# Dense router scores among the opening products, and balancing sums in the other bank

## The chip, the cores and the metric

The kernel runs on one core of one Trainium2 chip. The metric is the device time of one execution in microseconds, here the median of several runs. PE is TensorE's matmul side, PEld its weight loads, DVE is VectorE, ACT is ScalarE, POOL is GpSimd, SP is the engine that issues the weight DMAs.

## What is computed

Three stages follow one another: linear attention with a decaying state, a first mixture of experts in which each token takes one expert, and a second, dense mixture (`moe2`) in which every token takes all eight experts, weighted by a matrix P that is balanced over rows and columns eight times:

```python
def _moe2_ref(x, w_gate, w1, w2) -> np.ndarray:
    N, D = x.shape
    E = w_gate.shape[1]
    logits = x @ w_gate
    logits = logits - logits.max()
    P = np.exp(logits)
    for _ in range(8):
        P /= P.sum(1, keepdims=True) + 1e-09
        P /= P.sum(0, keepdims=True) + 1e-09
        P *= N / E
    out = np.zeros((N, D), dtype=np.float32)
    for e in range(E):
        h = np.maximum(x @ w1[e], 0.0)
        ye = h @ w2[e]
        out += P[:, e:e + 1] * ye
    return out.astype(np.float32)
```

Here N is 1536, D 512, E 8 and F (the inner size) 1024. `logits` are the dense router's scores; the change concerns how they, and then P, are made.

## The kernel before

The order of work is written by hand: each engine runs its instructions in the order in which the code issues them, and a wait is put where one engine needs another's result. Attention and the first mixture end with the slots of the first mixture (`rest_slot`). The transposed result x stands in two tiles, `x2T[0]` (high parts) and `x2T[1]` (low parts), so that each product of float32 quality is three matmuls: high by high, high by low, low by high (`product`, four blocks of 128 rows of D, so twelve matmuls of 384 columns, lines 780 to 782).

The dense mixture works in groups: half of the tokens, one expert, a quarter of F. Group 0 is `opening`: four products (z = 0 to 3) into banks 6 and 7 of PSUM in turn (`pa`, `pc`), each followed by a `relu` (ACT at line 785, then DVE at line 786) that writes the inner activations `hb`. `opening` stands in both branches of a conditional on the number of slots; the short branch is the one that ran here, and every engine then jumps over the other branch. Groups 1 to 3 are run by `eight`: four steps z, each one product, its `relu`, and then three "triples" of the group before (nine matmuls of 512 columns, lines 969 to 971, which multiply `hb` by the second weights and add up in banks 0 to 5). From group 4 on `seven` does the same with fewer products.

After `opening` the code issues the last weight conversions of expert 0: `conv1(7)` (ACT, then DVE, then a DMA on SP that fetches the second weights into the same staging tile `stg[7]`), then `conv2(4)` to `conv2(7)`, each an ACT copy (line 297) and a DVE difference (line 298). `conv2(7)` needs that DMA. Then come the loads of later weights (line 910) and the dense router:

- `gate_scores(c)`, c = 0 to 2: eight matmuls of 512 columns (line 817) into bank c, and an ACT copy (line 818) of 16 rows into `lgT`, which lies on the tile `snap`.
- `gate_exp`, behind step z = 0 of group 1: twelve "folds" (line 823), matmuls with 16 rows of weights and 8 columns that add high and low scores and turn them into token rows in bank 5. Each is float32 and runs as two passes, so 24 weight loads and 24 matmuls. Then DVE copies them to `Pm` (line 824) and takes the maximum of each row (line 825).
- `gate_peak` (line 829), behind step z = 1: a matmul that turns the maxima into a row, and a DVE maximum.
- `gate_shift` (line 834), behind step z = 2: spreads the maximum; DVE subtracts, ACT takes the exponential, and `balance_rows` (four DVE operations, lines 840 to 843) normalizes rows.
- `balance` (line 849), once behind each step of groups 2 and 3, eight times: a matmul of `ones` by `Pm` (two passes of 96 columns) that writes the column sums into columns 0 to 95 of the bank whose product the step has just made, four DVE operations (lines 850 to 853), and `balance_rows` but for the last.

POOL's first work after the slots is `xwhole` (line 866), sums of x blocks into `snap`. `points` is the table that says what runs behind which step of which group.

Of the kernel before, what the change touches and what calls it, by code (L numbers as in the profile page):

```python
# [15 lines left out]
AF = mybir.ActivationFunctionType  # L16
# [5 lines left out]
C = 128  # L22
NCH = S // C
M = B * NCH
# [92 lines left out]
def build(tc, i, out):  # L117
# [3 lines left out]
    with ctx:  # L121
# [523 lines left out]
        with ExitStack() as st2:  # L645
# [132 lines left out]
            def product(b, w, x, start, stop, kks=2):  # L778
                for kk in range(kks):
                    T.matmul(out=b, lhsT=w(0, kk), rhs=x(0, kk), start=start and kk == 0, stop=False, skip_group_check=True)  # L780
                    T.matmul(out=b, lhsT=w(0, kk), rhs=x(1, kk), start=False, stop=False, skip_group_check=True)  # L781
                    T.matmul(out=b, lhsT=w(1, kk), rhs=x(0, kk), start=False, stop=stop and kk == kks - 1, skip_group_check=True)  # L782

# [5 lines left out]

            def opening():  # L790
                for z in range(4):
                    fi, th = z % 2, z // 2
                    b = (pa, pc)[z % 2][:, 0:HT]
                    product(b, lambda t, kk: w1b[fi][:, t, kk], lambda t, kk: x2T[t][:, kk, th * HT:(th + 1) * HT], True, True, 4)
                    relu(hs[0][fi][th], b)
# [14 lines left out]
            lgT = snap.rearrange("p u t -> p (u t)")[0:2 * NE]  # L810
            rs, cs, gm = tab[:, 430:430 + M], tab[:, 446:446 + NE], tab[:, 458:460]
            ones12 = [128, M, NE]
            def gate_scores(c):
                b = bank[c]
                for t in range(2):
                    for kk in range(4):
                        T.matmul(out=b, lhsT=wg2s[:, kk], rhs=x2T[t][:, kk, c * 512:(c + 1) * 512], start=t == 0 and kk == 0, stop=t == 1 and kk == 3)
                A.activation(out=lgT[:, c * 512:(c + 1) * 512], in_=b[0:2 * NE], func=AF.Copy)

            def gate_exp():  # L820
                b = bank[5]
                for m in range(M):
                    T.matmul(out=b[:, m * NE:(m + 1) * NE], lhsT=lgT[:, m * C:(m + 1) * C], rhs=k("fold")[0:2 * NE], start=True, stop=True)
                V.tensor_copy(out=Pm, in_=b[:, 0:M * NE].rearrange("p (m e) -> p m e", e=NE))
                V.tensor_reduce(out=gm[:, 0:1], in_=Pm, axis=AX.XY, op=ALU.max)
# [21 lines left out]
            def balance(at):  # L847
                b = at[:, 0:M * NE]
                T.matmul(out=b, lhsT=ones, rhs=Pm.rearrange("p m e -> p (m e)"), start=True, stop=True)
                V.tensor_reduce(out=cs, in_=b.rearrange("p (m e) -> p e m", e=NE), axis=AX.X, op=ALU.add)  # L850
                V.tensor_scalar(out=cs, in0=cs, scalar1=1e-9, scalar2=None, op0=ALU.add)
                V.reciprocal(out=cs, in_=cs)
                V.scalar_tensor_tensor(out=Pm, in0=Pm, scalar=float(N) / NE, in1=bc(cs, 1, ones12), op0=ALU.mult, op1=ALU.mult)
                left[0] -= 1
                if left[0]:
                    balance_rows()
# [122 lines left out]
            def eight(n, points):  # L979
# [9 lines left out]
                for z, (fi, th) in enumerate(((0, 0), (1, 0), (0, 1), (1, 1))):  # L989
# [4 lines left out]
                    for _ in range(3):  # L994
                        for fn in (next(todo, None),):
                            if fn:
                                fn()
                    if old and z in (1, 3):
# [13 lines left out]
            def seven(n):  # L1012
# [52 lines left out]
                1: {0: [gate_exp], 1: [gate_peak], 2: [gate_shift]},  # L1065
            }
            for n in range(2, 4):
                points[n] = {z: [lambda z=z: left[0] and balance((pa, pc)[z % 2])] for z in range(4)}
# [11 lines left out]
            for c in range(3):  # L1080
                gate_scores(c)
# [27 lines left out]
```

## Time and profile before

| what | value |
|---|---|
| runs before, us | 1259.06, 1260.19, 1259.06 (median 1259.06) |
| profiled execution, us | 1260.48 |
| its span, us | 1258.7 |
| mean granted TensorE clock | 0.998 of full speed |
| PE busy | 1246.2 us, 99% |
| DVE, ACT, POOL busy | 678.4, 490.9, 423.3 us |
| chain that ended last | PE 96%, DVE 1%, DMA 1%, POOL 1%, issue 1% |

The span is what the trace of the one profiled execution covers; that execution's own time is 1.8 us longer, since some time lies around it. A busy PE is not PE at its peak: matmuls overlap, so the start of one to the start of the next is the measure of what it costs. The stretch of this change lies between 226 and 305 us.

### The profile page before, as it was taken

To read this page: it belongs to the slowest core of one execution; us is meant where nothing else is said; L and a number is where in the kernel's file an instruction comes from. 1 tells how busy PE (TensorE), PEld (TensorE's weight loads), DVE (VectorE), ACT (ScalarE), POOL (GpSimd) and SP (SyncE) were. 2 spreads that over 40 slices of the span, in tenths; PEclk is the share of its full clock that TensorE was granted. 3 is DMA by queue.
4 is the path that set the end of the run, shared out by engine and by line. 5 is a ranking of instruction groups with operands and counts; after the bars stand their busy time and mean duration, and the time that the engine had idled before them with its cause. 6 is when DMAs were issued, how large, how long until landed. Compare 5 with 4: busy or idle time off the path is not lost.

```text
span 1258.7 us, 19258 instructions
## 1 busy us (share of the span) xinstructions
PE 1246.2 (99%) x7284; PEld 1133.8 (90%) x7284; DVE 678.4 (54%) x1319; ACT 490.9 (39%) x981; POOL 423.3 (34%) x411
## 2 busy tenths in 40 slices
PE   8999999999999999999999999999999999999998
PEld 7899999889999999999999999999999999999996
DVE  7787777346545454545454546354545454545453
ACT  2344555313333333444444433343333333333331
POOL 5401010153333333333333347133333333333332
PEclk9999999999999999999999999999999999999999
DMA  8933655301222222222222232122222222222201
GB/s 311 303 115 121 209 183 160 112 1 42 68 67 68 67 68 67 67 67 67 68 68 67 67 101 85 58 68 71 68 70 68 67 65 71 67 67 68 67 26 51
DMA packets 56841, 112.47 MB, mean 89 GB/s; under 512 B 7088, under 2 KB 7344, under 8 KB 56736
## 3 DMA queue, kind: packets, MB, share of 16 engines
q1 hardware_dynamic: 52272, 100.89, 26.1%
q0 software_dynamic: 2304, 7.05, 1.7%
q10 hardware_dynamic: 2160, 3.18, 0.7%
q8 instruction: 60, 0.98, 0.3%
q14 instruction: 45, 0.37, 0.1%
HBM read 104.80 MB, written 6.29 MB: 88 GB/s over the span
## 4 chain that ended last, share of the span: by engine, by line
PE 96%; DVE 1%; DMA 1%; POOL 1%; issue 1%; ACT 0%; POOLq 0%; SPq 0%; DVEq 0%; ACTq 0%
PE banks L971 14%; PE banks L970 14%; PE banks L969 14%; PE banks L781 13%; PE banks L780 13%; PE banks L782 13%; PE banks L327 2%; PE banks L329 2%; PE banks L328 2%; PE banks L657 2%; PE banks L656 2%; PE banks L658 2%; PE banks L524 1%; PE banks L398 1%; PE banks L473 1%; PE banks L503 1%
## 5 line engine op out<-in xcount | busy, mean ns | idle before, releaser
L933 POOL TENSOR_TENSOR w1r<-sraw,w1r 128x1024 fp32r<-128x1024 f32 x56 | 134.5, 2401 | 573.8 <-ACT w1r L932 573.8
L971 PE MATMUL banks<-w2r,hb 128*128 128x512 f32 x750 | 294.8, 393 | 0.0
L970 PE MATMUL banks<-w2r,hb 128*128 128x512 f32 x750 | 294.1, 392 | 0.0
L969 PE MATMUL banks<-w2r,hb 128*128 128x512 f32 x750 | 291.6, 389 | 0.0
L971 PEld LDWEIGHTS banks<-w2r,hb 128*128 128x128 f32 x750 | 140.7, 188 | 29.6
L785 ACT ACTIVATE hb<-snap 128x384 fp32r<-128x384 f32 x168 | 87.8, 523 | 201.8 <-DVE snap L1055 120.1
L780 PE MATMUL banks<-x2T,w1r 128*128 128x384 f32 x464 | 158.1, 341 | 0.0
L970 PEld LDWEIGHTS banks<-w2r,hb 128*128 128x128 f32 x750 | 140.6, 188 | 19.3
L781 PE MATMUL banks<-x2T,w1r 128*128 128x384 f32 x464 | 157.9, 340 | 0.0
L969 PEld LDWEIGHTS banks<-w2r,hb 128*128 128x128 f32 x750 | 140.8, 188 | 19.0
L782 PE MATMUL banks<-x2T,w1r 128*128 128x384 f32 x464 | 156.6, 337 | 0.0
L782 PE MATMUL banks<-xt,w1r 128*128 128x384 f32 x448 | 151.1, 337 | 0.0
L780 PE MATMUL banks<-xt,w1r 128*128 128x384 f32 x448 | 150.8, 337 | 0.0
L781 PE MATMUL banks<-xt,w1r 128*128 128x384 f32 x448 | 150.8, 337 | 0.0
L786 DVE SCALAR_TENSOR_TENSOR hb<-snap,hb 128x384 fp32r<-128x384 f32 x168 | 102.7, 611 | 66.4 <-ACT hb L785 66.4
L786 DVE SCALAR_TENSOR_TENSOR hb<-banks,hb 128x384 fp32r<-128x384 f32 x88 | 49.0, 556 | 158.7 <-ACT hb L785 158.7
L785 ACT ACTIVATE hb<-banks 128x384 fp32r<-128x384 f32 x88 | 43.3, 492 | 211.4 <-PE banks L782 209.6
L298 DVE TENSOR_TENSOR w2r<-stg,w2r 128x512 fp32r<-128x512 f32 x150 | 103.4, 691 | 4.8 <-ACT w2r L297 4.7
L297 ACT ACTIVATE w2r<-stg 128x512 fp32r<-128x512 f32 x150 | 93.2, 623 | 3.4 <-DMA stg<-in_w_dram 3.4
L781 PEld LDWEIGHTS banks<-x2T,w1r 128*128 128x128 f32 x464 | 87.3, 188 | 5.5
L780 PEld LDWEIGHTS banks<-x2T,w1r 128*128 128x128 f32 x464 | 87.3, 188 | 5.5 <-issue 0.2
L781 PEld LDWEIGHTS banks<-xt,w1r 128*128 128x128 f32 x448 | 84.1, 188 | 7.3
(228 smaller groups left out, 2086.5 us busy)
## 6 DMA issues: line engine op xcount, KB each, us to landing
stg<-in_w_dram SPq DMA_DIRECT2D x333, 256.0 KB, 2.7
pk<-in_pack_dram SPq DMA_DIRECT2D x24, 512.0 KB, 6.6
xs<-xr ACTq DMA_DIRECT2D x12, 256.0 KB, 5.8
xrow<-in_w_dram SPq DMA_DIRECT2D x3, 256.0 KB, 5.6
xrow<-xs,gidx POOLq DMA_INDIRECT x21, 3.7
out_dram<-oacc,tokmap POOLq DMA_INDIRECT x12, 2.7
cst<-in_cst_dram SPq DMA_DIRECT2D x1, 109.0 KB, 7.6
pre<-in_pre_dram SPq DMA_DIRECT2D x1, 71.0 KB, 1.9
```

What stands on the lines that cost most here:

```text
L297: A.activation(out=dst[:, 0], in_=src, func=AF.Copy)
L298: eng.tensor_tensor(out=dst[:, 1], in0=src, in1=dst[:, 0].bitcast(F32), op=ALU.subtract)
L327: T.matmul(out=b, lhsT=w[:, 0, kk], rhs=xhl(0, kk), start=kk == 0, stop=False)
L780: T.matmul(out=b, lhsT=w(0, kk), rhs=x(0, kk), start=start and kk == 0, stop=False, skip_group_check=True)
L781: T.matmul(out=b, lhsT=w(0, kk), rhs=x(1, kk), start=False, stop=False, skip_group_check=True)
L782: T.matmul(out=b, lhsT=w(1, kk), rhs=x(0, kk), start=False, stop=stop and kk == kks - 1, skip_group_check=True)
L785: A.activation(out=h[:, 0], in_=src, func=AF.Relu)
L786: V.scalar_tensor_tensor(out=h[:, 1], in0=src, scalar=0.0, in1=h[:, 0].bitcast(F32), op0=ALU.max, op1=ALU.subtract)
L933: G.tensor_tensor(out=ws[:, 1], in0=sraw, in1=ws[:, 0].bitcast(F32), op=ALU.subtract)
L969: T.matmul(out=bank[mi], lhsT=h[:, 0, tok], rhs=w[:, 0], start=first, stop=False, skip_group_check=True)
L970: T.matmul(out=bank[mi], lhsT=h[:, 0, tok], rhs=w[:, 1], start=False, stop=False, skip_group_check=True)
L971: T.matmul(out=bank[mi], lhsT=h[:, 1, tok], rhs=w[:, 0], start=False, stop=last, skip_group_check=True)
```

## The change

The scores move into `opening`: `gate_scores(z)` stands ahead of product z for z = 0 to 2, and `product` takes a list of functions that it calls between its blocks. Products 1, 2 and 3 each get four folds (`gate_fold`), one behind each three matmuls. `lgT` moves from `snap` to the tile `xrow[0]`. `gate_exp` keeps the DVE copy and maximum alone and is issued ahead of group 1; `gate_peak` and `gate_shift` move up by one step, to z = 0 and z = 1 of group 1. `balance` now runs behind the first of the three triples of a step, in columns 384 to 479 of the bank that the step has not used, from z = 3 of group 1 to z = 2 of group 3.

```diff
-            def product(b, w, x, start, stop, kks=2):
+            def product(b, w, x, start, stop, kks=2, between=()):
                 for kk in range(kks):
...
                     T.matmul(out=b, lhsT=w(1, kk), rhs=x(0, kk), start=False, stop=stop and kk == kks - 1, skip_group_check=True)
+                    for fn in between[kk:kk + 1]:
+                        fn()
...
+            lgT = xrow[0].rearrange("p q d -> p (q d)")[0:2 * NE]
+
+            def gate_scores(c):
+                b = bank[c]
+                for t in range(2):
+                    for kk in range(4):
+                        T.matmul(out=b, lhsT=wg2s[:, kk], rhs=x2T[t][:, kk, c * 512:(c + 1) * 512], start=t == 0 and kk == 0, stop=t == 1 and kk == 3)
+                A.activation(out=lgT[:, c * 512:(c + 1) * 512], in_=b[0:2 * NE], func=AF.Copy)
+
+            def gate_fold(m):
+                T.matmul(out=bank[5][:, m * NE:(m + 1) * NE], lhsT=lgT[:, m * C:(m + 1) * C], rhs=k("fold")[0:2 * NE], start=True, stop=True)
+
             def opening():
                 for z in range(4):
+                    if z < 3:
+                        gate_scores(z)
                     fi, th = z % 2, z // 2
                     b = (pa, pc)[z % 2][:, 0:HT]
-                    product(b, lambda t, kk: w1b[fi][:, t, kk], lambda t, kk: x2T[t][:, kk, th * HT:(th + 1) * HT], True, True, 4)
+                    folds = [lambda m=m: gate_fold(m) for m in range(4 * z - 4, 4 * z)] if z else ()
+                    product(b, lambda t, kk: w1b[fi][:, t, kk], lambda t, kk: x2T[t][:, kk, th * HT:(th + 1) * HT], True, True, 4, folds)
                     relu(hs[0][fi][th], b)
...
             def gate_exp():
-                b = bank[5]
-                for m in range(M):
-                    T.matmul(out=b[:, m * NE:(m + 1) * NE], lhsT=lgT[:, m * C:(m + 1) * C], rhs=k("fold")[0:2 * NE], start=True, stop=True)
-                V.tensor_copy(out=Pm, in_=b[:, 0:M * NE].rearrange("p (m e) -> p m e", e=NE))
+                V.tensor_copy(out=Pm, in_=bank[5][:, 0:M * NE].rearrange("p (m e) -> p m e", e=NE))
...
             def balance(at):
-                b = at[:, 0:M * NE]
+                b = at[:, HT:HT + M * NE]
...
-                    for _ in range(3):
+                    for u in range(3):
                         for fn in (next(todo, None),):
                             if fn:
                                 fn()
+                        if u == 0 and z in sums.get(n, ()):
+                            balance((pa, pc)[(z + 1) % 2])
...
-                1: {0: [gate_exp], 1: [gate_peak], 2: [gate_shift]},
+                1: {0: [gate_peak], 1: [gate_shift]},
             }
-            for n in range(2, 4):
-                points[n] = {z: [lambda z=z: left[0] and balance((pa, pc)[z % 2])] for z in range(4)}
+            sums = {1: (3,), 2: range(4), 3: range(3)}
...
-            for c in range(3):
-                gate_scores(c)
+            gate_exp()
```

How the order of instructions changes at three places. First PE inside `opening` of the changed kernel, from the end of `gate_scores(1)` into product z = 1. `wg2s` are the score weights, `cst` holds the fold pattern, `xrow` is `lgT`; L798 is a score, L802 a fold, L780 to L782 a product.

```order
L798 MATMUL banks<-x2T_938,wg2s 128x512 x4
L798 MATMUL banks<-x2T_939,wg2s 128x512 x4
L780 MATMUL banks<-x2T_938,w1r 128x384
L781 MATMUL banks<-x2T_939,w1r 128x384
L782 MATMUL banks<-x2T_938,w1r 128x384
L802 MATMUL banks<-cst,xrow_115 128x8 [waits DMASW5_49,DMASW7_49,DMASW3_49,DMAHW2_49,DMASW1_49,Activation_49]
L780 MATMUL banks<-x2T_938,w1r 128x384
L781 MATMUL banks<-x2T_939,w1r 128x384
L782 MATMUL banks<-x2T_938,w1r 128x384
L802 MATMUL banks<-cst,xrow_115 128x8
```

Before, the twelve folds stood in one row behind step z = 0 of group 1; now each stands alone between product matmuls, twelve times.

Second, DVE behind the conditional, first before, then with the change. L298 are the differences of `conv1(7)` and of `conv2(4)` to `conv2(7)`; the last of them, from `stg_109`, waits for the DMA of `stg[7]`.

```order
L298 TENSOR_TENSOR w1r<-stg_109,w1r 128x512 [waits DMAHW2_49,PE_49,Activation_49]
L298 TENSOR_TENSOR w2r<-stg_106,w2r 128x512 [waits DMAHW6_49,Activation_49]
L298 TENSOR_TENSOR w2r<-stg_107,w2r 128x512 [waits DMAHW7_49,PE_49,Activation_49]
L298 TENSOR_TENSOR w2r<-stg_108,w2r 128x512 [waits DMAHW0_49,PE_49,Activation_49]
L298 TENSOR_TENSOR w2r<-stg_109,w2r 128x512 [waits DMAHW1_49,PE_49,Activation_49]
L786 SCALAR_TENSOR_TENSOR hb_936<-banks,hb_936 128x384 [waits DVE_49,Activation_49]
L824 COPY Pm<-banks 128x96 [waits PE_49]
L825 TENSOR_REDUCE tab<-Pm 128x1 [waits DVE_49]
```

```order
L298 TENSOR_TENSOR w1r<-stg_109,w1r 128x512 [waits DMAHW2_49,PE_49,Activation_49]
L298 TENSOR_TENSOR w2r<-stg_106,w2r 128x512 [waits DMAHW6_49,Activation_49]
L298 TENSOR_TENSOR w2r<-stg_107,w2r 128x512 [waits DMAHW7_49,PE_49,Activation_49]
L298 TENSOR_TENSOR w2r<-stg_108,w2r 128x512 [waits DMAHW0_49,PE_49,Activation_49]
L298 TENSOR_TENSOR w2r<-stg_109,w2r 128x512 [waits DMAHW1_49,PE_49,Activation_49]
L831 COPY Pm<-banks 128x96 [waits PE_49]
L832 TENSOR_REDUCE tab<-Pm 128x1 [waits DVE_49]
L788 SCALAR_TENSOR_TENSOR hb_936<-banks,hb_936 128x384 [waits Activation_49]
```

The copy and the maximum stand one place earlier, still behind all five differences, and on PE `gate_peak`, which needs the maximum, now stands here, behind step z = 0 of group 1:

```order
L976 MATMUL banks<-w2l,hb_932 128x512
L977 MATMUL banks<-w2l,hb_932 128x512
L978 MATMUL banks<-w2l,hb_932 128x512
L836 MATMUL banks<-gtab,tab 1x128 [waits DVE_49]
L780 MATMUL banks<-x2T_938,w1r 128x384
```

Between the jump and this L836 stand twelve product matmuls and nine of triples on PE; before, there stood 24 scores, two products, the triples of both steps and the folds.

Third, PE in a step of group 2 with the change: L856 is the balancing sum, L976 to L978 a triple.

```order
L976 MATMUL banks<-w2r,hb_937 128x512
L977 MATMUL banks<-w2r,hb_937 128x512
L978 MATMUL banks<-w2r,hb_937 128x512
L856 MATMUL banks<-Pm,ones 128x96 [waits DVE_49]
L976 MATMUL banks<-w2l,hb_936 128x512
L977 MATMUL banks<-w2l,hb_936 128x512
L978 MATMUL banks<-w2l,hb_936 128x512
L976 MATMUL banks<-w2r,hb_937 128x512
L977 MATMUL banks<-w2r,hb_937 128x512
L978 MATMUL banks<-w2r,hb_937 128x512
L780 MATMUL banks<-x2T_938,w1r 128x384 [waits DVE_49]
```

Before, the sum stood behind the third triple, and the product behind it had no wait of its own.

## Rows read from the trace of the kernel before

**Rows 1.** The page's part 1: busy time and share of each engine.

```profile
PE 1246.2 (99%) x7284; PEld 1133.8 (90%) x7284; DVE 678.4 (54%) x1319; ACT 490.9 (39%) x981; POOL 423.3 (34%) x411
```

**Rows 2.** Waits of the whole span: who waited for whom, total us, times, longest.

```profile
POOL snap L866 <- PE banks L823: 56.6, 1, 56.6
...
PE banks L969 <- ACT snap L818: 1.0, 1, 1.0
...
PE banks L849 <- DVE hb L786: 0.8, 2, 0.6
```

**Rows 3.** Timeline of PE, opening to folds: start, us, engine line op out<-in [idle before].

```profile
226.23 0.34 PE L780 MATMUL banks<-x2T,w1r 128*128 128x384 f32 x1
...
234.49 0.34 PE L782 MATMUL banks<-x2T,w1r 128*128 128x384 f32 x1
235.50 5.85 PE L817 MATMUL banks<-x2T,wg2s 128*128 128x512 f32 x24 [0.67 <-ACT hb L785]
241.19 0.33 PE L780 MATMUL banks<-x2T,w1r 128*128 128x384 f32 x1
...
246.44 0.40 PE L971 MATMUL banks<-w2l,hb 128*128 128x512 f32 x1
...
249.82 0.34 PE L781 MATMUL banks<-x2T,w1r 128*128 128x384 f32 x1
```

**Rows 4.** Windows of 1 us: length, busy of PE, PEld, DVE, ACT, POOL, granted clock, DMA.

```profile
251.00:252.00 1.00, 1.00 (x5) 1.00 (x4) 0.00 (x0) 0.00 (x0) 0.92 (x2) 0.50 0.00 0
...
254.00:255.00 1.00, 1.00 (x5) 0.76 (x5) 0.00 (x0) 0.00 (x0) 0.92 (x2) 0.86 0.00 0
...
1252.00:1253.00 1.00, 0.66 (x3) 0.19 (x2) 0.39 (x2) 0.00 (x0) 0.70 (x2) 1.00 0.50 188
...
1257.00:1258.00 1.00, 0.00 (x0) 0.00 (x0) 0.00 (x0) 0.00 (x0) 0.00 (x0) 0.89 0.00 0
```

**Rows 5.** Timeline of PE around `gate_peak` (L829), `gate_shift` (L834) and a plain step.

```profile
255.50 0.38 PE L829 MATMUL banks<-gtab,tab 128*1 128x128 f32 x2
...
256.09 0.34 PE L781 MATMUL banks<-x2T,w1r 128*128 128x384 f32 x1
...
259.87 0.40 PE L971 MATMUL banks<-w2l,hb 128*128 128x512 f32 x1
...
260.79 0.34 PE L781 MATMUL banks<-x2T,w1r 128*128 128x384 f32 x1
...
264.96 0.34 PE L781 MATMUL banks<-x2T,w1r 128*128 128x384 f32 x1
```

**Rows 6.** Timeline of weight loads: the folds.

```profile
246.77 2.75 PEld L823 LDWEIGHTS banks<-cst,snap 16*128 16x128 f32 x24 [0.36 <-issue]
```

**Rows 7.** Timelines of ACT and of DVE behind the opening.

```profile
234.93 0.49 ACT L785 ACTIVATE hb<-banks 128x384 fp32r<-128x384 f32 x1 [1.68 <-PE banks L782]
237.75 0.63 ACT L297 ACTIVATE w1r<-stg 128x512 fp32r<-128x512 f32 x1 [2.33 <-issue]
...
243.32 0.63 ACT L297 ACTIVATE w2r<-stg 128x512 fp32r<-128x512 f32 x1 [3.38 <-DMA stg<-in_w_dram]
...
238.56 0.69 DVE L298 TENSOR_TENSOR w1r<-stg,w1r 128x512 fp32r<-128x512 f32 x1 [2.56 <-ACT w1r L297]
...
243.98 0.69 DVE L298 TENSOR_TENSOR w2r<-stg,w2r 128x512 fp32r<-128x512 f32 x1 [2.92 <-ACT w2r L297]
...
249.65 0.26 DVE L824 COPY Pm<-banks 128x96 f32<-128x96 f32 x1 [3.30 <-PE banks L823]
249.94 0.25 DVE L825 TENSOR_REDUCE tab<-Pm 128x1 f32<-128x96 f32 x1
```

**Rows 8.** Timeline of PE around the first balancing sum.

```profile
268.74 0.39 PE L971 MATMUL banks<-w2l,hb 128*128 128x512 f32 x1
...
269.37 0.34 PE L781 MATMUL banks<-x2T,w1r 128*128 128x384 f32 x1
```

**Rows 9.** The page's part 6, DMA issues: how many, KB each, median us to landing.

```profile
stg<-in_w_dram SPq DMA_DIRECT2D x333, 256.0 KB, 2.7
```

More of the change, by code (lines that the diff above doesn't have):

```diff
@@ L809, in build @@
             oacc = []
-            lgT = snap.rearrange("p u t -> p (u t)")[0:2 * NE]
             rs, cs, gm = tab[:, 430:430 + M], tab[:, 446:446 + NE], tab[:, 458:460]
             ones12 = [128, M, NE]
[L813 to L818, printed above, removed]
             def gate_exp():
-                b = bank[5]
-                for m in range(M):
-                    T.matmul(out=b[:, m * NE:(m + 1) * NE], lhsT=lgT[:, m * C:(m + 1) * C], rhs=k("fold")[0:2 * NE], start=True, stop=True)
-                V.tensor_copy(out=Pm, in_=b[:, 0:M * NE].rearrange("p (m e) -> p m e", e=NE))
+                V.tensor_copy(out=Pm, in_=bank[5][:, 0:M * NE].rearrange("p (m e) -> p m e", e=NE))
                 V.tensor_reduce(out=gm[:, 0:1], in_=Pm, axis=AX.XY, op=ALU.max)
```

## The prediction, made before the changed kernel ran

> **What bounds the kernel now.** I read the busy shares first: PE is busy 99% of the span [rows 1], so the time is the length of PE's stream, and only what lengthens or shortens that stream counts. Next the waits of PE: they come to a few microseconds, and the ones in the stretch of the change are the first triple (L969), 1.0 us, held by ACT's copies of the scores, and two balancing sums, 0.8 us, held by DVE [rows 2]. Then PE's timeline from the opening on. The 48 products of the opening start between 226.23 and 234.49, 8.26 us; the next matmul, the first score, starts 1.01 us behind the last of them; the 24 scores take 5.69 us (235.50 to 241.19) [rows 3]. Last, the granted clock: it stands at full speed except for a drop that follows the row of folds (0.50 in the second from 251, 0.86 in the one from 254, and as low in between) [rows 4]. Half speed is 1.2 GHz, full speed 2.4 GHz.
>
> So the stretch holds some 6 us that are not matmul work. The question is which of it goes, and what waits in its place.
>
> **The sum, from one landmark to the same landmark.** I compare the start of the opening with the second matmul of the product that follows step z = 1 of group 1. Before it lies at 256.09 [rows 5], 29.86 us behind 226.23. Both kernels have done the opening, scores, folds, `gate_peak` and two steps by then.
>
> *Opening.* Products and scores cost what they cost: 8.26 and 5.69 us. Moving the scores saves no matmul; their 24 weight loads and three ACT copies move along, and the copies find ACT idle. A fold is dearer alone than in a row. The burst runs from the last triple (246.44) to the second matmul of the next product (249.82), 3.38 us [rows 3]. Two plain steps there would take 0.40 (21 matmuls of a plain step take 4.17, from 260.79 to 264.96 [rows 5]). The 24 passes begin at 246.77 and their loads take 2.75 in all [rows 6], 0.115 each; so entering and leaving the folds costs 3.38 - 2.75 - 0.40 = 0.23 beyond plain steps. A single fold pays that each time: 2 x 0.115 + 0.23 = 0.46, say 0.44, since the passes' ends overlap. Bounds: a balancing sum, two passes with all 128 rows, costs 269.37 - 268.74 - 0.40 = 0.23 [rows 8]; `gate_shift`, two passes with one row, costs 260.79 - 259.87 - 0.40 = 0.52 [rows 5]. I take 0.44: the fold's 16 rows resemble the 1 row, and its first load too starts only after PEld stood idle for 0.36 us [rows 6]. Eleven folds stand ahead of the opening's last product matmul, 4.84 us. So that matmul, which I call E, starts at 226.23 + 8.26 + 5.69 + 4.84 = 245.02.
>
> The row shows a load of 16-row weights that doesn't start under the matmul ahead of it. The Trainium skill, "TensorEngine Tiling (Array Packing)", Key Properties, has a rule for it: changing the tiling mode drains TensorE. By that rule the change turns two changes of mode into twenty-four, and the folds cost 12 x 0.44 = 5.3 us in place of 3.0; without it they would cost 12 x 0.23 = 2.8. The trace so far is on the rule's side, since the balancing sum's full-size load shows no such idle time.
>
> *From E to `gate_peak`.* Here the cover is gone. Before, from E = 234.49, ACT ends the last relu, jumps over the other branch and starts `conv1(7)` at 237.75 (2.33 us idle), DVE follows at 238.56, only then SP fetches `stg[7]`, ACT takes it at 243.32 and DVE ends it at 243.98 + 0.69 = 244.67 [rows 7]. That is E + 10.18, and nothing in the change touches a link of it. The 24 scores and a product hid it but for the last microsecond. Now DVE's copy to `Pm` (0.26) and row maximum (0.25) [rows 7] stand behind it in the queue, and `gate_peak` needs them: it starts at E + 10.8 at the earliest. PE has, between E and there, a fold, the jump and one step (4.17), 5.6 us with the old gap of 1.0. So PE waits for some 5.2 us. The wait of 1.0 on the score copies and the gap are swallowed by it. Behind the waiting matmul stands all of PE; the relu of z = 0, behind `conv2(7)` on ACT, ends on DVE half a microsecond after the maximum, before product z = 2 needs its bank.
>
> *Landmark.* 245.02 + 10.83 = 255.85; from `gate_peak` to the second matmul behind it 0.59 (255.50 to 256.09); then a plain step, 4.17 [rows 5]: 260.61, against 256.09. The difference is **+4.5**.
>
> *Clock.* The drop before is inside the 29.86 (three windows at 0.50 and one at 0.86: some 1.6 us lost [rows 4]) and goes with the burst. But a wait of 5 us is itself idle. After the last matmuls, in the window from 1252, PE does nothing and the clock falls in the window from 1257 [rows 4]: some 5 us of nothing bring 1.2 GHz. I put the price of the new drop at the old one's, **+1.5**, with 0 and 2.5 as ends: part of a drop may fall into the wait, where it costs nothing, or it may last through more work. The Trainium skill, "TensorE: Matmul & The Clock Gate", section "Why this matters for your kernels", says that idle gaps between bursts of matmuls bring the half rate back; by that alone the drop is certain, and the sum stands as it is.
>
> *Sums.* Their matmuls stay, eight, at 0.23 each. Their two waits of 0.8 us [rows 2] came from DVE, whose relu had to free the bank; in the other bank's spare columns they need only `Pm`, and a step later than before at that: **-0.8** (0 to -1.3, since a wait also empties PE's pipeline). In exchange each next product waits until DVE has read the sums in its bank; DVE reads them behind its relu, while PE has two more triples, 1.4 us, to do, so I cost that at nothing; if DVE were over a microsecond late it would show as a wait at L780.
>
> *Others at nothing.* POOL's first sums waited 56.6 us for the folds, through `snap` [rows 2]; they now start with the opening's end, and nobody waits for them before group 2. DVE, ACT and SP keep their order elsewhere.
>
> Sum: 4.5 + 1.5 - 0.8 = **+5.2 us**. The profiled execution took 1260.48, its span 1258.7; the median is 1.4 below it, and I add the difference to the median: 1259.06 + 5.2 = 1264.3. A measurement here can tell about 0.2%, 2.5 us, from no change.
>
> **Rivals.**
> 1. *The folds are cheap.* If their loads slip under the matmuls as the balancing sum's do (0.23), E comes 2.3 us earlier: +2.9, 1262.0; with a drop that falls wholly into the wait, +1.4, 1260.5. For it: burst passes take only 0.115 each. Against it: the idle 0.36 [rows 6].
> 2. *`gate_peak` doesn't wait.* The chain from E to the maximum would have to shrink from 10.8 to 5.6 us; the fetch of `stg[7]`, from 239.25 to 243.32 [rows 7], is the one soft link: 4.1 us where this line's median is 2.7 [rows 9], and faster starts behind the jump would be needed too. Then the wait of 5.2 and the new drop both go: 5.2 - 5.2 - 1.5 = -1.5, **1257.6**; with cheap folds as well, 1255.3. Against it: every link is in the order as before. The point from which it decides: DVE's last L298 ending before E + 5.0.
> 3. *The opening itself loses the clock.* With a fold of 0.44 behind each 0.52 us of products, PE does light work for almost half of three stretches, and a row of folds was what preceded the drop before. One such drop adds 1.6: 1265.9; two, 1267.5. Against it: the scores between are dense.
> 4. *The bank's wait bites*, so that each product stands until DVE has read the sums: seven times some 0.4, +2.8, 1267.1.
>
> **How the numbers follow.** Forecast 0.60, rivals 0.16, 0.10, 0.11 and 0.03. Slower by over 2.5 us: nearly all of the forecast (0.57), a third of rival 1 (0.06), rivals 3 and 4: 0.77. Within it: 0.03, 0.10 and 0.04 of rival 2: 0.17. Faster: the rest of rival 2, 0.06. The range: below, rival 1 with some of a faster fetch, 1260.8; above, the forecast with folds at 0.52 (+0.9) and the clock at its upper end (+1.0), which also takes in one drop of rival 3: 1266.6. What is left out is mostly rival 2 and the far ends of 3 and 4.
>
> **What would show it.** In the changed kernel's profile: a wait of 5 us at L836, released by DVE's L832 behind the last L298; twelve folds, each of which makes some 0.8 us of the start of the product matmul ahead of it to the start of the second one behind it (0.35 without a fold); no wait at the first triple; a clock window of 0.50 behind L836 and none behind the folds; fewer waits at L856 than at L849 before. The prediction is wrong if L836 starts without a wait, or if the folds add less than 0.3 each.

## The result and the profile after

The changed kernel takes 1267.17 us (median of 5 runs, 1266.83 to 1268.34) against 1259.69 us for the kernel before beside it (5 runs, 1259.06 to 1261.13): a ratio of 1.0061 with a 95% interval of 1.0046 to 1.0076, slower by 5.8 to 9.6 us. It is slower, as forecast, but by more than forecast: 1264.3 was predicted, with 1266.6 as the upper end. The profiled execution took 1266.83 us (span 1265.1), 6.35 more than the profiled one before.

Line numbers moved with the change: scores L798 (were L817), folds L802 (L823), DVE's copy and maximum L831 and L832 (L824, L825), `gate_peak` L836 (L829), `gate_shift` L841 (L834), sums L856 (L849), `balance`'s DVE operations L857 to L860 (L850 to L853), `balance_rows` L847 to L850 (L840 to L843), `relu` L787 and L788 (L785, L786), triples L976 to L978 (L969 to L971), POOL's sums L873 (L866).

The waits of the whole span, against [rows 2]: the wait on the score copies is gone, one at a sum is left, and the largest wait of PE is new. POOL's first sums no longer wait for the folds.

```profile
POOL snap L873 <- DVE hb L788: 50.2, 3, 40.7
...
PE banks L836 <- DVE tab L832: 3.8, 1, 3.8
...
PE banks L856 <- DVE Pm L850: 0.5, 1, 0.5
```

PE's timeline, against [rows 3, 5]: the start of the opening, one of the folds inside it, E (246.32), `gate_peak` behind its wait, the first matmuls of the product behind it, and `gate_shift`.

```profile
226.83 0.86 PE L798 MATMUL banks<-x2T,wg2s 128*128 128x512 f32 x3
...
233.06 0.34 PE L782 MATMUL banks<-x2T,w1r 128*128 128x384 f32 x1
233.33 0.38 PE L802 MATMUL banks<-cst,xrow 16*128 16x8 f32 x2
233.64 0.44 PE L780 MATMUL banks<-x2T,w1r 128*128 128x384 f32 x1
233.92 0.34 PE L781 MATMUL banks<-x2T,w1r 128*128 128x384 f32 x1
...
246.32 0.34 PE L782 MATMUL banks<-x2T,w1r 128*128 128x384 f32 x1
...
255.93 0.38 PE L836 MATMUL banks<-gtab,tab 128*1 128x128 f32 x2 [3.76 <-DVE tab L832]
256.24 0.56 PE L780 MATMUL banks<-x2T,w1r 128*128 128x384 f32 x1
256.59 0.52 PE L781 MATMUL banks<-x2T,w1r 128*128 128x384 f32 x1
...
262.17 0.38 PE L841 MATMUL banks<-tab,ones 1*128 1x1 f32 x2
262.48 0.45 PE L780 MATMUL banks<-x2T,w1r 128*128 128x384 f32 x1
262.76 0.34 PE L781 MATMUL banks<-x2T,w1r 128*128 128x384 f32 x1
```

A fold makes 0.86 us of the start of the matmul ahead of it to the second one behind it (233.06 to 233.92), where a plain row takes 0.35: 0.51 for one fold. E lies 19.49 us behind the start. Behind `gate_peak` the product's matmuls start 0.32 to 0.35 us apart instead of 0.17, and last 0.52 instead of 0.34: PE runs at half clock (1.2 GHz). The windows of 1 us (columns as in [rows 4], the granted clock third from the end) show it; the clock is 1.00 in every window of the opening and up to 256, so the folds alone brought no drop this time.

```profile
255.00:256.00 1.00, 0.07 (x1) 0.08 (x2) 0.97 (x4) 0.07 (x1) 0.00 (x0) 1.00 0.79 250
256.00:257.00 1.00, 1.00 (x5) 0.78 (x6) 0.61 (x2) 0.00 (x0) 0.00 (x0) 0.70 0.94 365
...
258.00:259.00 1.00, 1.00 (x5) 1.00 (x4) 0.00 (x0) 0.00 (x0) 0.00 (x0) 0.50 1.02 391
```

ACT and DVE behind the opening, against [rows 7]: the same links in the same order, with the copy and maximum as the last.

```profile
249.50 0.63 ACT L297 ACTIVATE w1r<-stg 128x512 fp32r<-128x512 f32 x1 [2.25 <-issue]
...
254.06 0.63 ACT L297 ACTIVATE w2r<-stg 128x512 fp32r<-128x512 f32 x1 [2.37 <-DMA stg<-in_w_dram]
...
250.44 0.69 DVE L298 TENSOR_TENSOR w1r<-stg,w1r 128x512 fp32r<-128x512 f32 x1 [2.60 <-ACT w1r L297]
...
254.72 0.69 DVE L298 TENSOR_TENSOR w2r<-stg,w2r 128x512 fp32r<-128x512 f32 x1 [1.27 <-ACT w2r L297]
255.33 0.25 DVE L831 COPY Pm<-banks 128x96 f32<-128x96 f32 x1
255.62 0.25 DVE L832 TENSOR_REDUCE tab<-Pm 128x1 f32<-128x96 f32 x1
```

For what comes behind `gate_shift` I take ACT's copy in group 4 that follows the second product there (L1039 before, L1048 after) as a second landmark.

```profile
306.03 0.49 ACT L1039 ACTIVATE snap<-banks 128x384 f32<-128x384 f32 x1 [0.26 <-PE banks L782]
```

```profile
312.38 0.49 ACT L1048 ACTIVATE snap<-banks 128x384 f32<-128x384 f32 x1 [1.24 <-PE banks L782]
```

From the second product matmul behind `gate_shift` to it: 306.03 - 260.79 = 45.24 before [rows 5], and one step more (4.17) belongs to it after, since `gate_shift` moved up by one: 49.41. After: 312.38 - 262.76 = 49.62. So the sums, which were to give 0.8 us, cost 0.21. From there to the last matmul both take 946.24 us.

| term | forecast | measured |
|---|---|---|
| ahead of the change (226.23 to 226.83) | 0 | +0.60 |
| start of the opening to E | 18.79 | 19.49 |
| E to `gate_peak` | 10.83 | 9.61 |
| clock behind `gate_peak` | +1.5 | +1.54 |
| sums | -0.8 | +0.21 |
| profiled execution against profiled execution | +5.2 | +6.35 |

The clock's term is `gate_peak` to the second product matmul behind `gate_shift`, 6.83 us after against 5.29 before [rows 5]. The differences to the forecast, 0.60 + 0.70 - 1.22 + 0.04 + 1.01 = 1.13, give the 1.15 by which the profiled execution is longer than 1260.48 + 5.2.

### The profile page after: what moved, and what is told of

It reads as the page before. It is cut to its first block, busy times and chain, and to the rows that moved or that the text cites. A ratio compares the mean times of both kernels' runs of the same rounds, so it can differ in the third digit from the quotient of the medians.

```text
span 1265.1 us, 19257 instructions
## 1 busy us (share of the span) xinstructions
PE 1250.4 (99%) x7284; PEld 1135.2 (90%) x7284; DVE 678.9 (54%) x1319; ACT 491.2 (39%) x981; POOL 423.4 (33%) x411
## 3 DMA queue, kind: packets, MB, share of 16 engines
q10 hardware_dynamic: 2160, 3.18, 0.7%
## 4 chain that ended last, share of the span: by engine, by line
PE 95%; DVE 2%; DMA 1%; issue 1%; POOL 1%; ACT 0%; POOLq 0%; SPq 0%; DVEq 0%; ACTq 0%
PE banks L978 14%; PE banks L977 14%; PE banks L976 13%; PE banks L780 13%; PE banks L781 13%; PE banks L782 12%; PE banks L327 2%; PE banks L329 2%; PE banks L328 2%; PE banks L657 2%; PE banks L656 2%; PE banks L658 2%; PE banks L398 1%; PE banks L524 1%; PE banks L473 1%; PE banks L503 1%
## 5 line engine op out<-in xcount | busy, mean ns | idle before, releaser
L978 PE MATMUL banks<-w2r,hb 128*128 128x512 f32 x750 | 294.8, 393 | 0.0
L976 PE MATMUL banks<-w2r,hb 128*128 128x512 f32 x750 | 292.0, 389 | 0.0
L978 PEld LDWEIGHTS banks<-w2r,hb 128*128 128x128 f32 x750 | 140.7, 188 | 29.6
L787 ACT ACTIVATE hb<-snap 128x384 fp32r<-128x384 f32 x168 | 87.7, 522 | 200.5 <-DVE snap L1064 120.2
L780 PE MATMUL banks<-x2T,w1r 128*128 128x384 f32 x464 | 159.0, 343 | 0.8 <-issue 0.7
L976 PEld LDWEIGHTS banks<-w2r,hb 128*128 128x128 f32 x750 | 140.8, 188 | 18.9
L782 PE MATMUL banks<-x2T,w1r 128*128 128x384 f32 x464 | 156.8, 338 | 0.0
L782 PE MATMUL banks<-xt,w1r 128*128 128x384 f32 x448 | 151.1, 337 | 0.0
L780 PE MATMUL banks<-xt,w1r 128*128 128x384 f32 x448 | 150.8, 337 | 0.0
L788 DVE SCALAR_TENSOR_TENSOR hb<-banks,hb 128x384 fp32r<-128x384 f32 x88 | 49.0, 557 | 173.1 <-ACT hb L787 173.1
L788 DVE SCALAR_TENSOR_TENSOR hb<-snap,hb 128x384 fp32r<-128x384 f32 x168 | 103.2, 614 | 66.3 <-ACT hb L787 66.3
L787 ACT ACTIVATE hb<-banks 128x384 fp32r<-128x384 f32 x88 | 43.2, 491 | 212.9 <-PE banks L782 203.7
L298 DVE TENSOR_TENSOR w2r<-stg,w2r 128x512 fp32r<-128x512 f32 x150 | 103.6, 692 | 3.6 <-ACT w2r L297 3.0
L780 PEld LDWEIGHTS banks<-x2T,w1r 128*128 128x128 f32 x464 | 87.5, 189 | 7.4 <-issue 1.0
```

Source lines behind the costliest of these rows:

```text
L298: eng.tensor_tensor(out=dst[:, 1], in0=src, in1=dst[:, 0].bitcast(F32), op=ALU.subtract)
L787: A.activation(out=h[:, 0], in_=src, func=AF.Relu)
L788: V.scalar_tensor_tensor(out=h[:, 1], in0=src, scalar=0.0, in1=h[:, 0].bitcast(F32), op0=ALU.max, op1=ALU.subtract)
L976: T.matmul(out=bank[mi], lhsT=h[:, 0, tok], rhs=w[:, 0], start=first, stop=False, skip_group_check=True)
L978: T.matmul(out=bank[mi], lhsT=h[:, 1, tok], rhs=w[:, 0], start=False, stop=last, skip_group_check=True)
```

## The experiments

From here on "from the start to `gate_shift`" means from the first matmul of the opening to the second product matmul behind `gate_shift`: 35.93 us in the changed kernel, 34.56 before (a step of 4.17 later in the program there). "To group 4" means from there to ACT's copy: 49.62 after. Times are medians beside runs of the kernel before on the same chip, whose median is given; it differs by chip. Behind the last matmul of the kernel PE is idle and the clock falls in every profile; where a text below says that no window is under 1.00, or adds up what the clock lost, that end is left out.

**e_exp_first: the copy and maximum ahead of the conversions.**

```
-            conv1(7, NE)
+            gate_exp()
+            conv1(7, NE)
...
-            gate_exp()
```

> The changed kernel with DVE's copy to Pm and row maximum put ahead of the last conversions of the slot (conv1(7), conv2(4..7)), so that gate_peak no longer stands behind the fetch of stg[7]. Theory 'wait': the 3.76 us at L836 and the clock drop behind it (1.7 us) are most of the loss: no wait at gate_peak, no window at half clock near it, 5.5 us less than the changed kernel, 1261.7 (2 us above the kernel before). Rival 'folds': the twelve single folds and their mode changes are the loss, the wait only moves to whatever stands next behind the same fetch: the time stays within 1.5 us of 1267.2.

Measured: 1261.32 (11 runs) against 1260.53, ratio 1.0005 (0.9996 to 1.0014). PE's timeline at `gate_peak`, and a window behind it:

```profile
251.18 0.40 PE L978 MATMUL banks<-w2l,hb 128*128 128x512 f32 x1
251.50 0.38 PE L836 MATMUL banks<-gtab,tab 128*1 128x128 f32 x2
251.81 0.44 PE L780 MATMUL banks<-x2T,w1r 128*128 128x384 f32 x1
```

```profile
253.00:254.00 1.00, 1.00 (x7) 1.00 (x6) 1.00 (x2) 0.00 (x0) 0.00 (x0) 1.00 0.92 330
```

No wait, no window under 1.00, and 30.16 us to `gate_shift`, 5.77 less than in the changed kernel (5.5 expected). The two small DVE operations in the wrong place of DVE's queue were worth nearly the whole loss: what is left against the kernel before is within the noise. The Trainium skill, "TensorE: Matmul & The Clock Gate", "Why this matters for your kernels", has idle gaps between bursts bring the half rate; the two runs agree: with the gap of 3.76 us the drop is there, without it not. A long gap isn't needed for a drop, though: the kernel before has one [rows 4] with no wait of PE over 1.03 us in this stretch.

**e_step_later: the wait covered instead of removed.** `gate_peak` and `gate_shift` a step later, the sums in groups 2 and 3.

```
-                1: {0: [gate_peak], 1: [gate_shift]},
+                1: {1: [gate_peak], 2: [gate_shift]},
...
-            sums = {1: (3,), 2: range(4), 3: range(3)}
+            sums = {2: range(4), 3: range(4)}
```

> The changed kernel with gate_peak and gate_shift a step later (z = 1 and z = 2 of group 1, as in the kernel before) and the eight sums behind them in groups 2 and 3; gate_exp stays behind the conversions. Theory 'cover': the wait of 3.76 us is there because the change put gate_peak one step (4.17 us) nearer to the opening; with that step back it goes whole, and the clock drop with it: 5.3 us less than the changed kernel, about the time of e_exp_first. Rival: the scores that no longer stand between E and the step are the missing cover too, so that 1 us or more of wait stays, and with it some of the clock drop: 2 to 4 us less.

Measured: 1261.51 (12 runs) against 1260.15, ratio 1.0013 (1.0005 to 1.0022); no wait at `gate_peak`, no window under 1.00. 'Cover' holds: 5.3 us less than the changed kernel's 1267.17 would be 1261.9, and in the profile it is 34.64 us to `gate_shift`, 5.46 less than the changed kernel's 35.93 plus the step of 4.17 by which `gate_shift` now stands later. The change took away two covers, the scores behind E and the step by which `gate_peak` moved up; the step alone, put back, is enough to hide the 3.76 us and to keep the clock.

**e_fours: the folds in rows of four.**

```
-                    for fn in between[kk:kk + 1]:
+                    for fn in between if kk == kks - 1 else ():
```

> The changed kernel with its folds in three rows of four, each behind a whole product, in place of one behind each quarter of a product. Theory 'entry price': a fold costs 0.115 for each of its two passes plus 0.28 us each time PE goes in and out of the folds, so three rows cost 3 x (4 x 0.23 + 0.28) = 3.6 us in place of 12 x 0.51 = 6.1: 2.5 us less than the changed kernel, 1264.7, with the wait at gate_peak still some 3.8 us. With the 0.115 a fold that the burst of twelve seemed to cost (row of passes overlapped), 4.1 less. Rival 'price of each': a fold costs 0.5 us wherever it stands: no difference (1267.2). If a row of four already brings the clock down, 1.6 us of the gain go again.

Measured: 1263.19 (11 runs) against 1260.53, ratio 1.0023 (1.0014 to 1.0032). PE's timeline at the first row:

```profile
234.40 0.34 PE L782 MATMUL banks<-x2T,w1r 128*128 128x384 f32 x1
234.67 1.05 PE L802 MATMUL banks<-cst,xrow 16*128 16x8 f32 x8
235.65 0.73 PE L798 MATMUL banks<-x2T,wg2s 128*128 128x512 f32 x2
```

The row takes 235.65 - 234.40 - 0.17 = 1.08, 0.27 a fold against 0.51 alone, so three rows cost 3.2 in place of 6.1; to `gate_shift` it is 32.24, 3.69 less than in the changed kernel (the third row stands behind E, where the wait hides it). 'Price of each' falls. The wait stays (3.1 us in the list), since `gate_peak` starts 9.41 behind E: it is tied to E, not to PE's work. It was 9.61, 9.21, 9.41 and 9.40 in the four profiles that have this wait.

**e_full_rows: what makes a single fold dear.**

```
-lhsT=lgT[:, m * C:(m + 1) * C], rhs=k("fold")[0:2 * NE]
+lhsT=ones, rhs=ones[:, 0:NE]
```

> The changed kernel with folds of the same number, place and columns, but with 128-row weights (ones times ones in place of the scores times the fold matrix, so the router's weights are left out). It measures the price of a single fold. If the 16 rows, a smaller piece of the array, are what makes a fold dear, a fold falls from 0.51 to the 0.23 of a balancing sum, the opening from 19.5 to 16.4 us, and the whole by some 3 us (or less, if the wait at gate_peak grows by a part). If any matmul that breaks the row of products costs this much, it stays at 0.5.

Measured: one run, 1264.41, against 1260.15. PE's timeline at its first fold:

```profile
232.90 0.34 PE L782 MATMUL banks<-x2T,w1r 128*128 128x384 f32 x1
233.07 0.28 PE L802 MATMUL banks<-ones 128*128 128x8 f32 x2
233.21 0.42 PE L780 MATMUL banks<-x2T,w1r 128*128 128x384 f32 x1
233.47 0.33 PE L781 MATMUL banks<-x2T,w1r 128*128 128x384 f32 x1
```

The fold's matmul now follows the product's by 0.17, as any other, and the fold costs 0.57 - 0.35 = 0.22, the price of a balancing sum (0.23). The opening to E fell from 19.49 to 16.33. So 0.29 of the 0.51 is the change to 16 rows and back. The weight loads show where it lies, first in the changed kernel, then here: with 16 rows PEld stands idle for 0.26 us ahead of the fold's load, with 128 rows it doesn't.

```profile
233.33 0.29 PEld L802 LDWEIGHTS banks<-cst,xrow 16*128 16x128 f32 x2 [0.26 <-issue]
```

```profile
232.90 0.36 PEld L802 LDWEIGHTS banks<-ones 128*128 128x128 f32 x2
```

The Trainium skill, "TensorEngine Tiling (Array Packing)", Key Properties, says that a change of the tiling mode drains TensorE. This pair of runs agrees with that if 16 rows of weights count as another mode, which no run here shows.

To `gate_shift` it is 33.68, only 2.25 less than in the changed kernel and not 3.1, since the clock lost twice as much (3.41 us against 1.71, added up over the windows): from `gate_peak` to the second product matmul behind `gate_shift` it took 7.95 us in place of 6.83. Why the drop was longer here wasn't tried. The clock is under 1.00 in eight windows, of which this is the second.

```profile
252.00:253.00 1.00, 0.60 (x3) 0.18 (x3) 0.77 (x3) 0.00 (x0) 0.00 (x0) 0.50 0.90 322
```

**e_exp_fours: both edits** (the two diffs above).

> The changed kernel with both edits: copy to Pm and row maximum ahead of the last conversions, and the folds in three rows of four. If the two prices are independent: 5.5 + 2.5 = 8.0 less than the changed kernel, 1259.2, as the kernel before; with the cheaper row of folds (4.1) 1257.6, some 2 us faster than before. If the clock falls behind the rows of folds, 1.6 us more.

Measured: 1258.95 (11 runs) against 1260.53, ratio 0.9993 (0.9984 to 1.0002). The time is the first value of the two expected, 27.85 to `gate_shift`, 8.08 less than in the changed kernel, with no window under 1.00. The two measured prices do not quite add up, though: 5.77 + 3.69 = 9.46. With the wait gone, nothing hides the third row of folds behind E any more (1.08 in place of 0.51) nor PE's wait at the jump (0.65 in place of 0.21).

**e_row12: all folds in one row behind the last product.**

```
-                    folds = [lambda m=m: gate_fold(m) for m in range(4 * z - 4, 4 * z)] if z else ()
+                    folds = [lambda m=m: gate_fold(m) for m in range(M)] if z == 3 else ()
```

> As e_exp_fours, but all twelve folds in one row behind the last product of the opening. The row costs 24 x 0.115 + 0.25 = 3.0 us by the burst of the kernel before, against 3 x 1.08 = 3.24 measured for three rows of four. Theory 'long row brings the clock down': 0.2 us less on PE, but a window at 0.50 within 5 us behind the row in most executions, 1.7 us, as behind the row of twelve in the kernel before: 1 to 1.5 us more than e_exp_fours. Rival: the drop has to do with what surrounds the row (the wait on the score copies, the jump): no drop, 0.2 less.

Measured: 1260.53 (12 runs) against 1260.15, ratio 1.0002 (0.9994 to 1.0011), some 1.1 us more than e_exp_fours by the ratios. To `gate_shift` 29.52, 1.67 more. The row starts at 241.39 and lasts 2.84; PE's next matmul and the windows behind it:

```profile
245.58 0.69 PE L780 MATMUL banks<-x2T,w1r 128*128 128x384 f32 x1 [1.34 <-issue]
```

```profile
245.00:246.00 1.00, 0.42 (x1) 0.43 (x2) 0.46 (x3) 0.96 (x2) 0.00 (x0) 0.76 0.03 8
246.00:247.00 1.00, 1.00 (x4) 1.00 (x4) 1.00 (x3) 1.00 (x3) 0.00 (x0) 0.50 0.09 25
```

The long row is followed by the drop in another place too, with the same jump behind it that three rows of four stand without loss. It seems to come in most executions: 11 of the 12 have a mean clock of 0.997 or less, 1 of 11 in e_exp_fours. But the row isn't alone here: PE stood idle for 1.34 us directly behind it, against 0.65 in e_exp_fours, and the clock fell about when that idle time ended. So the rival, what surrounds the row, is not ruled out.

**e_sums_only: the kernel before with the new sums.**

```
-                b = at[:, 0:M * NE]
+                b = at[:, HT:HT + M * NE]
...
+                        if u == 0 and n in (2, 3):
+                            balance((pa, pc)[(z + 1) % 2])
```

> The kernel before with nothing changed but the balancing sums: in the spare columns of the other bank and behind the first triple of the step. Forecast's term: 0.8 us less than the kernel before (0 to 1.3 less). Rival, read from the two traces (group 4 starts 0.2 us later relative to gate_shift than before): no gain, 0 to 0.3 us more, since the sum then waits for DVE's Pm, a chain that POOL's sums slow down, and not for the bank.

Measured: 1259.51 (11 runs) against 1260.53, ratio 0.9995 (0.9986 to 1.0004), which can't tell the two apart by itself. The trace can: to group 4 it took 45.52, 0.28 more than before (45.24), and the same stretch is steady from profile to profile (49.59 to 49.63 in seven that share the changed kernel's sums). The rival holds, and the term of 0.8 isn't there. This profile showed one thing more. Up to the sums it is the kernel before, with the same row of twelve folds (24 passes, 2.84 us), and yet no window is under 1.00; the one of [rows 4] at 251 reads here:

```profile
251.00:252.00 1.00, 1.00 (x7) 1.00 (x6) 0.00 (x0) 0.00 (x0) 0.92 (x2) 1.00 0.00 0
```

So the drop behind the folds does not come in every execution of the kernel before. The 33 executions of it that ran beside this kernel, e_exp_first, e_fours and e_exp_fours fit that: the 9 with a mean clock of 0.999 have a median of 1258.98, the 16 with 0.998 one of 1260.65, the 5 with 0.997 one of 1262.21 (3 at 0.996, 1261.04, stand outside that order). A mean clock is only a hint, since the idle end of the kernel lowers it too: the profile of e_step_later has 0.998 with no other drop.

**e_changed_again: the changed kernel beside more runs of before.**

> The changed kernel once more, beside more executions of the kernel before. By the theory, every execution of the changed kernel has the drop behind gate_peak (clock 0.998 or less), while the kernel before has one in about three of four: the difference of the medians is 6 to 7 us, and to those executions of before with a clock of 0.999 it is 8 us. Rival: the clock of before has nothing to do with its spread, and the difference is the same to all of them.

Measured: 1267.88 (5 runs, none with a clock above 0.998) against 1261.53 (21 runs): 6.4 by the medians, ratio 1.0054 (1.0039 to 1.0070), and 8.1 against the six executions of before with 0.999 (median 1259.79). Both numbers are as expected, so the rival falls.

**e_pool_early: POOL's work off the sums.** As e_exp_fours, with POOL's sums and splits in other places of the table.

```
-            for j, at, lag in ((0, 1, 2), (1, 32, 0)):
+            for z, fn in ((0, lambda: xwhole(0, 0)), (0, lambda: xsplit(0)), (1, lambda: xwhole(0, 1)), (3, lambda: xsplit(1))):
+                points[1].setdefault(z, []).append(fn)
+            for j, at, lag in ((1, 32, 0),):
```

> As e_exp_fours, but POOL's two rounds of sums and splits for the group that follows are issued two to five steps earlier, so that most of them are done before the balancing chain runs on DVE. Theory 'DVE's small operations are stretched while POOL works' (an 8-column tensor_scalar takes 1.05 us under POOL's sums and 0.17 without): the balancing chain of 4.5 us falls to 2.3, no wait at the balancing sums, and from gate_shift to group 4 it takes 0.7 to 1.0 us less (48.7 in place of 49.63). Rival: the sums lose at the product's bank or in their own passes, and this stays at 49.6; or gate_shift's own chain is stretched instead, and a first sum waits for it.

Measured: **1257.49** (9 runs) against 1260.15, ratio 0.9978 (0.9968 to 0.9987): 1.6 to 4.0 us faster than the kernel before, and so than both kernels of this study. To group 4 it takes 48.22, 1.41 less than e_exp_fours; more than the 1.0 expected. No wait at a sum is left. Here is why, from the changed kernel: DVE's chain behind its third sum, beside POOL's sums, and one of its operations behind a later sum, before POOL's next work.

```profile
278.43 2.02 POOL L873 TENSOR_TENSOR snap<-x2T,x2T 128x384 f32<-128x384 f32 x2
280.52 1.02 POOL L877 TENSOR_TENSOR snap<-snap 128x384 f32<-128x384 f32 x1
```

```profile
279.13 0.26 DVE L857 TENSOR_REDUCE tab<-banks 128x8 f32<-128x96 f32 x1
279.43 1.05 DVE L858 TENSOR_SCALAR tab<-tab 128x8 f32<-128x8 f32 x1
280.51 0.21 DVE L859 RECIPROCAL tab<-tab 128x8 f32<-128x8 f32 x1
280.75 0.91 DVE L860 SCALAR_TENSOR_TENSOR Pm<-Pm,tab 128x96 f32<-128x96 f32 x1
...
282.86 0.87 DVE L850 TENSOR_TENSOR Pm<-Pm,tab 128x96 f32<-128x96 f32 x1
283.65 0.55 DVE L788 SCALAR_TENSOR_TENSOR hb<-banks,hb 128x384 fp32r<-128x384 f32 x1
...
293.54 0.17 DVE L858 TENSOR_SCALAR tab<-tab 128x8 f32<-128x8 f32 x1
```

```profile
282.90 0.40 PE L978 MATMUL banks<-w2l,hb 128*128 128x512 f32 x1
283.78 0.46 PE L856 MATMUL banks<-Pm,ones 128*128 128x96 f32 x2 [0.48 <-DVE Pm L850]
```

An operation on 8 columns takes 1.05 us instead of 0.17; the chain takes 4.60 us (279.13 to 283.73), and with the relu of 0.55 in the same queue more than a step (4.41 from one undisturbed sum to the next). The sum that comes next has to wait for `Pm`, in whatever bank it writes. In e_pool_early the same chain behind the third sum takes 2.04 us (271.28 to 273.32); the two ahead of it, still beside POOL's work, take 3.5 each and fit into a step. The Trainium skill, "SBUF — State Buffer", "Who interferes with whom", lists which DVE instructions contend with GpSimd: those with two SBUF inputs when GpSimd reads SBUF, `tensor_scalar` in some cases, and not `tensor_reduce`. The rows agree: L858 (a `tensor_scalar`) and L860 (two SBUF inputs) stretch, the reduction (0.26) doesn't, nor does the reciprocal (0.21), which that list doesn't name.

**e_before_pool: the same alone, in the kernel before.**

```
-            for j, at, lag in ((0, 1, 2), (1, 32, 0)):
+            for n, z, fn in ((1, 0, lambda: xwhole(0, 0)), (1, 1, lambda: xsplit(0)), (1, 1, lambda: xwhole(0, 1)), (2, 0, lambda: xsplit(1))):
+                points[n].setdefault(z, []).append(fn)
+            for j, at, lag in ((1, 32, 0),):
```

> The kernel before with POOL's first split, second sums and second split for the group that follows issued three to four steps earlier, and nothing else. Theory 'DVE under POOL': its two waits of 0.76 us at the balancing sums go without any change of bank or place, 0.9 to 1.4 us less than the kernel before, all of it between gate_shift and group 4. Rival 'bank': the waits stay at 0.7 or more, since the relu still has to free the bank; no difference.

Measured: 1260.40 (11 runs) against 1261.53, ratio 0.9993 (0.9984 to 1.0002). Both waits at the sums are gone, with bank and place as they were, and to group 4 it takes 43.96, 1.28 less than before. 'DVE under POOL' holds, 'bank' falls. Not all of it reaches the time: the profile has the longer drop behind the folds (six windows at 0.50 from 250 on); 8 of its 11 executions have a mean clock of 0.997 or less, 5 of the 21 of before do, so the longer drop seems to come with this edit; by what means wasn't tried.

**e_sum_third: the sums behind the third triple, in the other bank.**

```
-                        if u == 0 and z in sums.get(n, ()):
+                        if u == 2 and z in sums.get(n, ()):
```

> As e_exp_fours, but the sums stand behind the third triple of their step, as in the kernel before, and stay in the spare columns of the other bank. Theory 'period': under POOL's work a sum's chain on DVE takes 4.1 to 4.6 us and a relu of 0.55 stands in the same queue, while a step is 4.4 us; the place inside the step doesn't matter, the third and fourth sum are late all the same, and from the product behind gate_shift to group 4 it stays at 49.4 to 49.8 us. Rival 'place': two more triples (1.4 us) of cover take the wait of 0.5 us away: 48.7 to 49.0, 0.7 us less than e_exp_fours.

Measured: 1263.12 (11 runs) against 1261.53, ratio 1.0015 (1.0006 to 1.0024), and 52.81 to group 4, 3.18 more than e_exp_fours. Both expectations missed it. The wait for `Pm` is gone indeed, but another took its place, the largest in PE's list (total, times, longest):

```profile
PE banks L780 <- DVE tab L857: 2.8, 8, 0.4
```

The next product goes into the bank whose spare columns hold the sum, so it stands until DVE has read it, eight times. This is the forecast's rival 4, with its price and the point from which it decides: with two triples between, as in the changed kernel, it costs nothing.

## Why the prediction was right in its sign and short in its size

**Right.** The wait at `gate_peak` came where and why it was forecast: released by L832 behind the last conversion, 9.61 behind E, with the clock drop behind it at the price taken (1.54 for 1.5). e_exp_first and e_step_later remove it in two ways, and nearly all of the loss goes with it. Rival 2 fell with the wait itself: DVE's last L298 ended at E + 9.1, not before E + 5.0. Rival 3 fell, since the opening kept its clock, rival 1 at 0.51 a fold, and rival 4, since no product waited for DVE to read a sum. That the clock's price came out so close has some luck in it: behind nearly the same wait, e_full_rows lost twice as much.

**Two terms were off, in opposite directions.** A fold measured 0.51, not 0.44: eleven of them 0.8 us more, of which 0.70 shows at E. The reason given for going below the 0.46, "since the passes' ends overlap", isn't borne out by the trace; the nearest row was `gate_shift`'s 0.52, the other price with few rows. And E to `gate_peak` was 1.22 shorter, since the conversions' last fetch landed about 1.1 us earlier behind E than in the one execution I had (2.9 us behind DVE's reading of `stg[7]`, not 4.1); that fetch was called the soft link, and its range should have been in the sum.

**Wrong: the sums, -0.8, measured +0.21.** The step that failed reads "came from DVE, whose relu had to free the bank; in the other bank's spare columns they need only `Pm`". The relu was the last to come, but it was late because it stood behind DVE's own chain, stretched by POOL. In the kernel before, ahead of the sum that waited longest:

```profile
277.55 0.88 DVE L843 TENSOR_TENSOR Pm<-Pm,tab 128x96 f32<-128x96 f32 x1
278.35 0.54 DVE L786 SCALAR_TENSOR_TENSOR hb<-banks,hb 128x384 fp32r<-128x384 f32 x1
```

```profile
278.95 0.46 PE L849 MATMUL banks<-Pm,ones 128*128 128x96 f32 x2 [0.58 <-DVE hb L786]
```

`Pm` comes out of that same chain, and so the new place waits for it: from the matmul ahead of the sum to the second one behind it, the fourth sum takes 1.44 us and the third 1.06, where a free one takes 0.69. e_sums_only shows the term alone, e_before_pool and e_pool_early its cause.

**Wrong: the median.** The other step that failed is "the median is 1.4 below it, and I add the difference to the median". It takes the changed kernel's median to lie 1.4 below its profiled execution too; it lay 0.34 above (1267.17 against 1266.83). These 1.76 us and the 1.15 by which the profiles differ from the sum are the whole 2.9 by which the forecast was short.

The likely reason, which the clocks bear out but don't prove: the profiled execution before had a clock drop behind its folds, and the sum counts it as gone in the change; two of the three runs before, at 1259.06, probably had none (their clocks aren't on record), as the executions at a clock of 0.999 run at about that time (1258.98, among the 33). The new drop behind `gate_peak`, by contrast, shows in both profiles of the changed kernel, and none of its ten executions has a clock above 0.998. Against the executions without the drop the same sum would have read 1.7 us more. With it and with the sums at nothing the forecast, in hindsight, is 1259.06 + 4.5 + 1.5 + 1.7 = 1266.8, where 1267.17 was measured. The range reached for dear folds and a long drop; it had neither of these two in it. Its upper end isn't what its parts give, either: 1264.3 + 0.9 + 1.0 = 1266.2, not 1266.6.

The 0.60 us ahead of the change remains: no instruction there moved, and the profiles differ there by up to 1.6 us (the opening starts between 226.23 and 227.84), so I count it as scatter.

## What to carry to other kernels

Before a consumer is moved up, follow its producer's queue: here two operations of 0.25 us stood behind a DMA fetch they had nothing to do with, and that, not the matmuls moved, made up nearly all of the loss: with the two out of the way the change is within the noise of the kernel before (ratio 1.0005, 0.9996 to 1.0014). A wait names the last link only; look at what that link stood behind, and at whether its operations take longer there than elsewhere in the same trace. And when a term of a sum is a clock drop, see first in the runs' clocks whether the median execution has it.

## What the runs showed of the chip that I had not expected

- The clock lost the same amount each time: added up over the windows (1 less the granted clock), 1.71 us in the kernel before, the changed kernel (both profiles), e_fours and e_row12, and 3.41 in e_full_rows and e_before_pool. No profile has a value between.
- A row of twelve 16-row folds, with PE never idle inside it, was followed by a drop in three of the four profiles with such a row (in e_before_pool by the long one); three rows of four were not. In e_row12 1.34 us of idle time came between, so the row alone isn't shown to be the cause.
- DVE's operation on 8 columns took six times as long (1.05 against 0.17 us) beside POOL's sums on other tiles.
- A pair of passes with 16 rows between full matmuls costs 0.51 us, with 128 rows 0.22; four pairs with 16 rows in a row cost 1.08.
